# An attention backward kernel: K of nearly all heads is transposed by DMA, and V is loaded a tick sooner

## The chip, the cores and the metric

The kernel runs on one core of a Trainium2 chip. The metric is the device time of one execution in microseconds (us); the time before is the median of three runs, 1652.15 us (1651.94 to 1654.73). A core has TensorE (PE, matrix products), VectorE (DVE), ScalarE (ACT), GpSimd (POOL) and SyncE (SP). In this kernel SyncE issues all DMA transfers, one after the other, in one queue; sixteen DMA engines carry them out.

## The reference: what is computed

Two independent attention blocks, A and B, each with 8 batch elements, 32 heads, 96 query tokens, 512 cached keys and a head width of 128. The model width is 640. Their outputs are concatenated, and the gradient of the whole is taken for every input:

```python
q = (x @ wq).reshape(B, Sq, H, Dh).transpose(0, 2, 1, 3)
scores = jnp.einsum("bhqd,bhkd->bhqk", q, k_cache) * (Dh ** -0.5)
p = softmax(scores, axis=-1)
o = jnp.einsum("bhqk,bhkd->bhqd", p, v_cache)
out = o.transpose(0, 2, 1, 3).reshape(B, Sq, H * Dh) @ wo      # block A and block B
result = concatenate([outA, outB], axis=-1)
_out, _vjp = jax.vjp(_f, A_x, A_k_cache, A_v_cache, A_wq, A_wo, B_x, ...)
return (_out, *_vjp(grad_out))          # out, and dx, dk, dv, dwq, dwo of both blocks
```

All arrays are bfloat16. The caches K and V and their gradients make up most of the traffic: per head and pair of batch elements 256 KB each of K, V, dK and dV.

## The kernel before, in words

**Units and ticks.** The work is cut into units of one head h and one batch element b, 8 units per head, 512 in all. A unit passes through stages s1 to s8, and the stages of successive units are overlapped like in a pipeline. Time is counted in ticks: unit (h, b) has the tick ct = tick0 + 8h + b, and each of its stages runs at ct plus an offset from the table `OFF` (line 45). An `Emitter` (lines 16 to 28) collects all pieces as (tick, slot, function), sorts them, and emits them in that order; the order in which the pieces are emitted is the order of each engine's instructions, save that the softmax stages s2 and s3 are given a higher priority. A tick of TensorE lasts some 2.6 to 3.9 us, depending on what the heads add to it.

**The stages.**
- Load (`c_ld`, line 262): K and V of a pair of batch elements come by one plain DMA each. `OFF["ldk"]` is -5, `OFF["ldv"]` is -3. A pair is loaded at the tick of its even element, so K and V loads fall on odd ticks.
- Transposes (`c_xt`, line 272): K (`KT`) and V (`VT`) of the pair are needed with the head dimension on the partitions too. A DMA through the crossbar writes the transposed copy from SBUF to SBUF, at `OFF["kt"]` = -3 and `OFF["vt"]` = 0. It waits for the load.
- s1 (`c_s1`, line 280, at ct + 2): for some units K is transposed by TensorE instead, in four 128x128 pieces into PSUM (line 285), and VectorE copies the result to SBUF as `KT_pe` (line 287). Which units is told by `k_on_pe` (line 556): batch elements 0 and 1 of every even head, all of head 0 of both blocks, and all of head 1 of the first block.
- s2 (line 291, ct + 3): the scores S = Q K^T (line 298), their negated maximum on VectorE (line 300), and the exponential on ScalarE (line 310). s3: reciprocal of the row sum on VectorE (line 320), and the product `P_sb` on GpSimd (line 329).
- s4 (ct + 4): dV = P^T dO on TensorE (line 389), copied out by ScalarE into `dV_sb`; P is transposed. s5: O. s6 (ct + 6): dP = dO V^T (line 417), and dS on VectorE (line 421). s7 (ct + 7): dK (line 432), copied out by ScalarE (line 435), and dS transposed. s8 (ct + 8): dQ from K as loaded (line 340).
- Stores (`c_st`, line 395): dV of a pair at its odd element's ct + 5, dK at its ct + 8.

Between these units the heads' own work is spread: transposes and projections of wq and wo (`pA` to `pD`), gradients of wq and wo (`qA` to `qD`), and per group of up to five heads the output and dx projections (`gU`, line 514). A head with `gU` work in it takes longer than one without.

**SyncE's order.** Of the emitted pieces, the DMAs come to SyncE in the order of tick and slot: loads in slot 0, transposes in slot 1, stores in 1.5, weights in 1.6 and 1.7. So an odd tick holds a V load, a K load, a K transpose (if DMA does it) and a dK store; an even tick holds a V transpose and a dV store. Each waits in that queue for its data and for its buffer: the K load, for instance, for the matmuls that read the buffer last, which are those of s8. Whatever stands behind it in the queue waits too.

**Buffers.** K_sb has 7 buffers (of a pair each), V_sb 5, KT and VT 4 each, KT_pe 2, P_sb 5, dS_sb 3. The eight PSUM banks are shared by all products.

Of the kernel before, what the change touches and what calls it, by code (L numbers as in the profile page):

```python
# [11 lines left out]
BF16 = mybir.dt.bfloat16  # L12
# [29 lines left out]
SL_GRP = 95  # L42
SL_SETUP = 96

OFF = dict(ldk=-5, ldv=-3, kt=-3, vt=0, s2=3, s3=3, s4=4, s5=5, s6=6, s7=7, s8=8)
HK = dict(pA=-10, pA2=-9, pB=-3, pC0=[-2, 0], pC1=[-1, 0], pD1=1, pD0=2, qA0=18, qA1=17, qB=[19, 20], qD=[(18, 0, 2), (19, 2, 4), (21, 4, 5)])
EV = dict(pB0="act", pB1="dve", pC00="act", pC01="act", pC10="act", pC11="dve", pD0="dve", pD1="dve", qA0="act", qA1="dve", qB0="act", qB1="dve", qD="dve", gU="act")
GSPREAD0 = 9
# [2 lines left out]
SLOTS = dict(LOAD=0, S2A=5, S2B=5.5, S1=6, S8=10, S7=20, S5=30, S4=40, S6=50, S3A=52, S3B=53, S5B=54, HEAD=SL_HEAD, GRP=SL_GRP)  # L51


def build_block(tc, em, tick0, blk, x, kc, vc, wq, wo, g_all, out_all, dx, dk, dv, dwq, dwo, ident, ones, pools, HG=6, first=True, groups=None):
    nc = tc.nc
    B, Sq, D = x.shape
    _, H, Sk, Dh = kc.shape
# [6 lines left out]
    NB = 2  # L64
# [31 lines left out]
    const, ps, kvp, wk, hd, hst, grp = (pools[k] for k in ("const", "ps", "kvp", "wk", "hd", "hst", "grp"))  # L96

    def bank(shape, dt, name):
        return ps.tile(shape, dt, name=name, tag="bank")
# [11 lines left out]
    def pinned(ins):  # L111
        return tc.keep_in_program_order(ins)
# [149 lines left out]
    def c_ld(h, b, n, bufs):  # L262
        def f():
            src = kc if n == "K" else vc
            X = kvp.tile([128, NB, KC, 128], BF16, name=n + "_sb", bufs=bufs)
            pinned(nc.sync.dma_start(X[:], src[b:b + NB, h].rearrange("b (p c) d -> p b c d", c=KC)))
            for i in range(NB):
                st = CS.setdefault((blk, h, b + i), {})
                st[n + "_sb"], st[n + "_all"] = X[:, i], X
        return f  # L270
# [9 lines left out]
    def c_s1(h, b):  # L280
        def f():
            st = CS[(blk, h, b)]
            kT_ps = bank([128, Sk], BF16, "kT_ps")
            for c in range(KC):
                nc.tensor.transpose(kT_ps[:, c * 128:(c + 1) * 128], st["K_sb"][:, c, :], ident[:])
            KT = wk.tile([128, Sk], BF16, name="KT_pe", bufs=2)
            nc.vector.tensor_copy(KT[:], kT_ps[:])
            st["KT"] = KT[:]
        return f

    def c_s2a(h, b):
        def f():
            with tc.high_priority(PRIO_OFF):
# [3 lines left out]
                S_ps = bank([Sq, Sk], F32, "S_ps")  # L297
                nc.tensor.matmul(S_ps[:], hs["QT_h"][:, tok], st["KT"], start=True, stop=True)  # L298
                negm = wk.tile([Sq, 1], F32, name="negm", bufs=3)
# [24 lines left out]
    def c_s3b(h, b):  # L324
        def f():
            with tc.high_priority(PRIO_OFF):
                st = CS[(blk, h, b)]
                P_sb = wk.tile([Sq, Sk], BF16, name="P_sb", bufs=5)
                pinned(nc.gpsimd.tensor_scalar(P_sb[:], st["E_sb"][:], st["rinv"][:], 0.0, op0=ALU.mult, op1=ALU.add))  # L329
                st["P_sb"] = P_sb  # L330
        return f
# [79 lines left out]
    def c_s6(h, b):  # L411
        def f():
            st = CS[(blk, h, b)]
            hs = HS[(blk, h)]
            tok = slice(b * Sq, (b + 1) * Sq)
            dP_ps = bank([Sq, Sk], F32, "dP_ps")
            nc.tensor.matmul(dP_ps[:], hs["dOT_h"][:, tok], st["VT"], start=True, stop=True)  # L417
            dl_ps = bank([Sq, 1], F32, "dl_ps")
            nc.tensor.matmul(dl_ps[:], st["prod"][:], ones[:, 0:1], start=True, stop=True)  # L419
            dS_sb = wk.tile([Sq, Sk], BF16, name="dS_sb", bufs=3)  # L420
            nc.vector.scalar_tensor_tensor(dS_sb[:], dP_ps[:], dl_ps[:, 0:1], st["P_sb"][:], op0=ALU.subtract, op1=ALU.mult)  # L421
            st["dS_sb"] = dS_sb
        return f
# [130 lines left out]
    NTS = len(tsplits)  # L554

    def k_on_pe(h, b):
        return (b // NB == 0 and h % 2 == 0) or h == 0 or (first and h == 1)

    SX = pools["SX"]
    for g in range(NG):  # L560
        h0 = GH0[g]
        for hh in range(groups[g]):
            h = h0 + hh
            c0t = tick0 + h * B
            if not (first and h == 0):
                em.add(c0t + HK["pA"], SLOTS["LOAD"] + 1.7, pA(h))
                em.add(c0t + HK["pA2"], SLOTS["LOAD"] + 1.7, pA2(h))
            em.add(c0t + HK["pB"], SL_HEAD, pB(h))
            fh = first and h == 0
            p0, p1, d1, d0, late = HK["pC0"], HK["pC1"], HK["pD1"], HK["pD0"], 0  # L570
            if fh:
                p1, d1, d0, late = [3, 3], 3, 4, 7
            elif h == 0:
                p0, p1, d1, d0, late = [-2, 2], [0, 3], 3, 4, 7
            for si in range(NTS):
                em.add(c0t + p0[min(si, 1)], SL_HEAD, pC(h, 0, si))
                em.add(c0t + p1[min(si, 1)], SL_HEAD + late, pC(h, 1, si))
            em.add(c0t + d1, SL_HEAD + (8 if late else 0), pD(h, 1))
            em.add(c0t + d0, SL_HEAD, pD(h, 0))
            for b in range(B):  # L580
                ct = c0t + b
                if b % NB == 0:
                    em.add(tick0 - 12 if first and h == 0 and b == 0 else ct + OFF["ldk"], SLOTS["LOAD"], c_ld(h, b, "K", 7))
                    em.add(ct + OFF["ldv"], SLOTS["LOAD"], c_ld(h, b, "V", 5))
                    if not k_on_pe(h, b):
                        em.add(ct + OFF["kt"], SLOTS["LOAD"] + 1, c_xt(h, b, "KT", 4))
                    em.add(ct + OFF["vt"], SLOTS["LOAD"] + 1, c_xt(h, b, "VT", 4))
                if k_on_pe(h, b):
                    em.add(ct + 2, SLOTS["S1"], c_s1(h, b))
                em.add(ct + OFF["s2"], SLOTS["S2A"], c_s2a(h, b))  # L590
                em.add(ct + OFF["s2"], SLOTS["S2B"], c_s2b(h, b))
                em.add(ct + OFF["s3"], SLOTS["S3A"], c_s3a(h, b))
                em.add(ct + OFF["s3"], SLOTS["S3B"], c_s3b(h, b))
                em.add(ct + OFF["s5"], SLOTS["S5B"], c_s5b(h, b))
                if b % 2 == 1:
                    em.add(ct + OFF["s4"] + 1, SLOTS["LOAD"] + 1.5, c_st(h, b, "v"))
                    em.add(ct + OFF["s7"] + 1, SLOTS["LOAD"] + 1.5, c_st(h, b, "k"))
                em.add(ct + OFF["s4"], SLOTS["S4"], c_s4(h, b))
                for i, o in enumerate(("s8", "s7", "s5", "s4")):
                    SX.setdefault(ct + OFF[o], [None] * 4)[i] = (blk, h, b)  # L600
                em.add(ct + OFF["s6"], SLOTS["S6"], c_s6(h, b))
                em.add(ct + OFF["s7"], SLOTS["S7"], c_s7(h, b))
            hk = HK if first or h < H - 1 else dict(HK, qA0=13, qB=[14, 15], qA1=16, qD=[(19, 0, 2), (19, 2, 4), (19, 4, 5)])
            em.add(c0t + hk["qA0"], SL_HEAD, qA(h, 0))
            for di in range(len(wsplits)):
                em.add(c0t + hk["qB"][di], SL_HEAD + 1, qB(h, di))
            em.add(c0t + hk["qB"][-1] + 1, SLOTS["LOAD"] + 1.6, qB_st(h))
            em.add(c0t + hk["qA1"], SL_HEAD, qA(h, 1))
            for (k_, c_lo, c_hi) in hk["qD"]:
                if c_lo < DC and h % 2 == 1:  # L610
                    em.add(c0t + k_, SL_HEAD + 2, qD(h, c_lo, min(c_hi, DC)))
            if h % 2 == 1:
                em.add(c0t + hk["qD"][-1][0] + 1, SLOTS["LOAD"] + 1.6, qD_st(h))
        cLg = tick0 + (h0 + groups[g] - 1) * B + B - 1
        gs0 = max(3, (GSPREAD0 * groups[g]) // HG)
        gs1 = max(3, (GSPREAD1 * groups[g]) // HG)
        if not first and g == NG - 2:
            gs0, gs1 = 9, 9
        if g == 0:
            em.add(cLg + OFF["s5"] - 2, SL_LOAD, setup_acc)  # L620
        subs = [(0, t, gi) for t in range(TT) for gi in range(len(gsplits))] + [(1, t, gi) for t in range(TT) for gi in range(len(gsplits))]
        n_out = TT * len(gsplits)
        for i, (which, t, gi) in enumerate(subs):
            if which == 0:
                tk = cLg + OFF["s5"] + 2 + (i * gs0) // n_out
            else:
                tk = cLg + OFF["s8"] + 2 + gs0 - 3 + ((i - n_out) * gs1) // n_out
            em.add(tk, SL_GRP, gU(g, which, t, gi))
            if g == NG - 1 and gi == len(gsplits) - 1:
                em.add(tk + 1, SLOTS["LOAD"] + 1.6, gU_st(which, t))  # L630
# [124 lines left out]
```

## Time and profile before

| | before |
|---|---|
| median of 3 runs | 1652.15 us (1651.94 to 1654.73) |
| the profiled execution | 1653.38 us, its span 1651.2 us |
| granted TensorE clock, mean | 0.998 |
| busy, us: PE / ACT / DVE / POOL | 1633.2 / 1391.9 / 1283.2 / 527.9 |
| moved by DMA | 447.11 MB, 271 GB/s |
| transposes by DMA | 256 of V, 214 of K |
| units with K transposed by TensorE | 84 |

The span runs from the first to the last instruction of the profiled execution. "Busy" is the time in which at least one instruction of the engine was under way. A row of a timeline has the start in us from the span's start, the duration in us, the engine, the line, the operation, and what it writes and reads; "x4" says that four were merged, and brackets tell idle time before it and what ended it. SPq is SyncE's queue: its duration is how long SyncE was held at that instruction, with any wait, not how long the transfer took. "To landing" is the time from the issue to the moment at which the data were there. Matmul durations hold the way through the array, so those of successive matmuls overlap. PEld are weight loads beside the matmuls.

### The profile page before, as it was taken

To read this page: it belongs to the slowest core of one execution; us is meant where nothing else is said; L and a number is where in the kernel's file an instruction comes from. 1 tells how busy PE (TensorE), PEld (TensorE's weight loads), DVE (VectorE), ACT (ScalarE), POOL (GpSimd) and SP (SyncE) were. 2 spreads that over 40 slices of the span, in tenths; PEclk is the share of its full clock that TensorE was granted. 3 is DMA by queue.
4 is the path that set the end of the run, shared out by engine and by line. 5 is a ranking of instruction groups with operands and counts; after the bars stand their busy time and mean duration, and the time that the engine had idled before them with its cause. 6 is when DMAs were issued, how large, how long until landed. Compare 5 with 4: busy or idle time off the path is not lost.

```text
span 1651.2 us, 55679 instructions
## 1 busy us (share of the span) xinstructions
PE 1633.2 (99%) x21288; PEld 1303.0 (79%) x21288; DVE 1283.2 (78%) x2916; ACT 1391.9 (84%) x3518; POOL 527.9 (32%) x1034
## 2 busy tenths in 40 slices
PE   8999999999999999999999999999999999999999
PEld 6887787788788787887878877877877877877886
DVE  6886677788787787878878767778878778787777
ACT  6998898798798797988869998978977977987985
POOL 2332233232233232333323323323322322332332
PEclk9999999999999999999999999999999999999999
DMA  9999999999999999999999999999999999999995
GB/s 258 270 268 283 277 284 271 279 274 283 246 277 269 276 273 264 267 278 259 299 289 283 283 281 272 278 281 271 276 275 260 278 296 246 282 282 245 265 275 157
DMA packets 843947, 447.11 MB, mean 271 GB/s; under 512 B 516512, under 2 KB 843680, under 8 KB 843680
## 3 DMA queue, kind: packets, MB, share of 16 engines
q1 hardware_dynamic: 843680, 443.56, 110.8%
q8 instruction: 167, 2.74, 0.7%
q14 instruction: 100, 0.82, 0.1%
HBM read 161.09 MB, written 159.12 MB: 194 GB/s over the span
## 4 chain that ended last, share of the span: by engine, by line
PE 74%; ACT 15%; issue 5%; DVE 3%; DMA 2%; POOL 0%; SPq 0%; ACTq 0%; DVEq 0%; POOLq 0%
PE o_ps L514 12%; PE q_ps L243 10%; PE dwq_ps L490 6%; PE dK_ps L432 5%; PE dV_ps L389 5%; PE dP_ps L417 5%; PE S_ps L298 5%; PE dwo_ps L469 4%; PE dst_ps L346 4%; PE x_ps L365 4%; PE x_ps L359 4%; PE x_ps L340 4%; ACT dK_sb L435 3%; ACT E_sb L310 3%; ACT PT_sb L378 3%
## 5 line engine op out<-in xcount | busy, mean ns | idle before, releaser
L329 POOL TENSOR_SCALAR P_sb<-E_sb,rinv 96x512 bf16<-96x512 bf16 x512 | 353.6, 691 | 1096.3 <-DVE rinv L320 1062.1
L310 ACT ACTIVATE E_sb<-S_ps,negm 96x512 bf16<-96x512 f32 x512 | 354.4, 692 | 132.7 <-DVE negm L300 128.9
L421 DVE SCALAR_TENSOR_TENSOR dS_sb<-dP_ps,dl_ps,P_sb 96x512 bf16<-96x512 f32 x512 | 380.9, 744 | 46.7 <-PE dl_ps L419 42.4
L300 DVE TENSOR_REDUCE negm<-S_ps 96x1 f32<-96x512 f32 x512 | 347.5, 679 | 46.0 <-PE S_ps L298 43.9
L435 ACT ACTIVATE dK_sb<-dK_ps 128x512 bf16<-128x512 f32 x512 | 305.7, 597 | 89.1 <-PE dK_ps L432 88.1
L392 ACT ACTIVATE dV_sb<-dV_ps 128x512 bf16<-128x512 f32 x512 | 314.6, 614 | 0.0
L378 ACT ACTIVATE PT_sb<-x_ps 128x384 bf16<-128x384 bf16 x512 | 256.4, 501 | 0.0
L514 PEld LDWEIGHTS <-OD 128*128 128x128 bf16 x1536 | 135.7, 98 | 103.3 <-issue 1.3
L389 PE MATMUL dV_ps<-dOnat_h,P_sb 96*128 96x128 bf16 x2048 | 197.9, 219 | 1.0 <-DVE dOnat_h L160 0.6
L432 PE MATMUL dK_ps<-Qnat_h,dS_sb 96*128 96x128 bf16 x2048 | 197.8, 219 | 0.0
L417 PE MATMUL dP_ps<-VT,dOT_h 128*96 128x512 bf16 x512 | 195.3, 381 | 0.3
L407 POOL TENSOR_TENSOR prod<-OD,dOT_h 128x96 bf16<-128x96 bf16 x512 | 186.6, 364 | 9.2 <-ACT OD L375 8.2
L348 DVE COPY dST_sb<-dst_ps 128x384 bf16<-128x384 bf16 x512 | 177.1, 346 | 11.6 <-PE dst_ps L346 11.6
L320 DVE RECIPROCAL rinv<-rowsum 96x1 f32<-96x1 f32 x512 | 80.0, 156 | 133.3 <-ACT E_sb L310 128.6
L375 ACT ACTIVATE OD<-x_ps 128x192 bf16<-128x192 f32 (+1 forms) x515 | 171.4, 333 | 3.4 <-PE x_ps L340 3.4
L346 PE MATMUL dst_ps<-ident,dS_sb 96*128 96x96 bf16 x2048 | 171.8, 206 | 2.4 <-DVE dS_sb L421 0.2
L359 PE MATMUL x_ps<-PT_sb,V_sb 128*128 128x96 bf16 x2048 | 172.2, 206 | 0.5 <-ACT PT_sb L378 0.5
L365 PE MATMUL x_ps<-ident,P_sb 96*128 96x96 bf16 x2048 | 171.7, 205 | 0.5 <-POOL P_sb L329 0.3
L340 PE MATMUL x_ps<-dST_sb,K_sb 128*128 128x96 bf16 x2048 | 170.7, 206 | 0.0
L298 PE MATMUL S_ps<-KT,QT_h 128*96 128x512 bf16 x428 | 162.1, 379 | 1.1 <-DMA KT<-K_sb 0.7
L340 PEld LDWEIGHTS <-K_sb 128*128 128x128 bf16 x2048 | 133.3, 98 | 34.6
L514 PE MATMUL o_ps<-wo_h,OD 128*128 128x128 bf16 (+1 forms) x768 | 141.0, 299 | 0.0
(75 smaller groups left out, 3137.9 us busy)
## 6 DMA issues: line engine op xcount, KB each, us to landing
out_dram<-dV_sb SPq DMA_DIRECT2D x256, 256.0 KB, 3.5
out_dram<-dK_sb SPq DMA_DIRECT2D x256, 256.0 KB, 3.8
K_sb<-in_A_k_cache_dram SPq DMA_DIRECT2D x128, 256.0 KB, 4.1
V_sb<-in_A_v_cache_dram SPq DMA_DIRECT2D x128, 256.0 KB, 3.8
K_sb<-in_B_k_cache_dram SPq DMA_DIRECT2D x128, 256.0 KB, 4.1
V_sb<-in_B_v_cache_dram SPq DMA_DIRECT2D x128, 256.0 KB, 4.0
out_dram<-dwo_sb SPq DMA_DIRECT2D x64, 160.0 KB, 3.8
out_dram<-dwq_sb SPq DMA_DIRECT2D x32, 320.0 KB, 4.0
```

What stands on the lines that cost most here:

```text
L300: nc.vector.tensor_reduce(negm[:], S_ps[:], axis=AX.X, op=ALU.max, negate=True)
L310: nc.scalar.activation(E_sb[:], st["S_ps"][:], ACT.Exp, bias=st["negm"][:], scale=1.0, accum_out=rowsum[:])
L329: pinned(nc.gpsimd.tensor_scalar(P_sb[:], st["E_sb"][:], st["rinv"][:], 0.0, op0=ALU.mult, op1=ALU.add))
L340: nc.tensor.matmul(dQT_ps, st["K_sb"][:, c, :], st["dST_sb"][:, c * Sq:(c + 1) * Sq], start=(c == 0), stop=(c == KC - 1))
L378: nc.scalar.activation(PT_sb[:], PT_ps, ACT.Identity, scale=1.0)
L389: nc.tensor.matmul(dV_ps[:, c * 128:(c + 1) * 128], P_sb[:, c * 128:(c + 1) * 128], hs["dOnat_h"][:, b * 128:(b + 1) * 128], start=True, s ...
L392: nc.scalar.activation(SB[(blk, h, b // 2, "v")][:, b % 2], dV_ps[:], ACT.Identity, scale=1.0)
L417: nc.tensor.matmul(dP_ps[:], hs["dOT_h"][:, tok], st["VT"], start=True, stop=True)
L421: nc.vector.scalar_tensor_tensor(dS_sb[:], dP_ps[:], dl_ps[:, 0:1], st["P_sb"][:], op0=ALU.subtract, op1=ALU.mult)
L432: nc.tensor.matmul(dK_ps[:, c * 128:(c + 1) * 128], dS_sb[:, c * 128:(c + 1) * 128], hs["Qnat_h"][:, b * 128:(b + 1) * 128], start=True, s ...
L435: nc.scalar.activation(SB[(blk, h, b // 2, "k")][:, b % 2], dK_ps[:], ACT.Identity, scale=1.0)
L514: nc.tensor.matmul(o_ps[:], src[:, t * 128:(t + 1) * 128], rhs, start=(hh == 0), stop=(hh == groups[g] - 1))
```

## The change

1. `k_on_pe` is cut down: TensorE transposes K only in head 0 of both blocks and in head 1 of the first. The two units of every other even head, which it transposed too, now get K by a DMA transpose, one more per even head.
2. V is loaded at ct - 4 instead of ct - 3, and V_sb has 6 buffers instead of 5. The V load now falls on an even tick. SyncE's order becomes: odd tick K load, K transpose, dK store; even tick V load, V transpose, dV store. So two plain transfers stand between any two transposes (weights and their gradients aside), where it was one and three.
3. KT_pe has 1 buffer instead of 2, P_sb 4 instead of 5, dS_sb 2 instead of 3.

```diff
-OFF = dict(ldk=-5, ldv=-3, kt=-3, vt=0, s2=3, s3=3, s4=4, s5=5, s6=6, s7=7, s8=8)
+OFF = dict(ldk=-5, ldv=-4, kt=-3, vt=0, s2=3, s3=3, s4=4, s5=5, s6=6, s7=7, s8=8)
...
-            KT = wk.tile([128, Sk], BF16, name="KT_pe", bufs=2)
+            KT = wk.tile([128, Sk], BF16, name="KT_pe", bufs=1)
...
-                P_sb = wk.tile([Sq, Sk], BF16, name="P_sb", bufs=5)
+                P_sb = wk.tile([Sq, Sk], BF16, name="P_sb", bufs=4)
...
-            dS_sb = wk.tile([Sq, Sk], BF16, name="dS_sb", bufs=3)
+            dS_sb = wk.tile([Sq, Sk], BF16, name="dS_sb", bufs=2)
...
     def k_on_pe(h, b):
-        return (b // NB == 0 and h % 2 == 0) or h == 0 or (first and h == 1)
+        return h == 0 or (first and h == 1)
...
-                    em.add(ct + OFF["ldv"], SLOTS["LOAD"], c_ld(h, b, "V", 5))
+                    em.add(ct + OFF["ldv"], SLOTS["LOAD"], c_ld(h, b, "V", 6))
```

## The prediction

> **What bounds the kernel now.** I read the page first, then the table of waits (last line: total us, times, longest), then TensorE's timeline, then SyncE's.
>
> ```profile
> span 1651.2 us, 55679 instructions
> PE 1633.2 (99%) x21288; PEld 1303.0 (79%) x21288; DVE 1283.2 (78%) x2916; ACT 1391.9 (84%) x3518; POOL 527.9 (32%) x1034
> PEclk9999999999999999999999999999999999999999
> ...
> PE 74%; ACT 15%; issue 5%; DVE 3%; DMA 2%; POOL 0%; SPq 0%; ACTq 0%; DVEq 0%; POOLq 0%
> ...
> PE S_ps L298 <- DMA KT<-K_sb: 0.7, 1, 0.7
> ```
>
> TensorE is busy for 99% of the span and carries 74% of the chain; the clock is granted in full, and TensorE waited for a K transpose only once. So TensorE is the bound, and a matmul taken away is worth its slot in TensorE's stream. The slot is not the duration that a group shows, because the durations overlap. It is the distance to the next start (columns: start in us, duration):
>
> ```profile
> 203.88 0.39 PE L285 MATMUL kT_ps<-ident,K_sb 128*128 128x128 bf16 x4
> 204.10 0.25 PE L340 MATMUL x_ps<-dST_sb,K_sb 128*128 128x96 bf16 x2
> ...
> L285 PE MATMUL kT_ps<-ident,K_sb x336: 216/219/219, 12.1 to 1574.2; 128*128 128x128 bf16 x168
> L287 DVE COPY KT_pe<-kT_ps x84: 397/408/425, 12.5 to 1575.5; 128x512 bf16<-128x512 bf16 x84
> ```
>
> Four transposes for one batch element lie 204.10 - 203.88 = 0.22 us in front of the next work, not 4 x 0.219 us.
>
> Behind TensorE stands a second line of work that is nearly as long: SyncE's one queue. The starts of the first K load of heads 8, 9, 10, 11 and 12 in that queue are these:
>
> ```profile
> 184.24 0.44 SPq L266 DMA_DIRECT2D K_sb<-in_A_k_cache_dram  x1
> 208.24 0.44 SPq L266 DMA_DIRECT2D K_sb<-in_A_k_cache_dram  x1
> 233.54 0.45 SPq L266 DMA_DIRECT2D K_sb<-in_A_k_cache_dram  x1
> 257.69 0.45 SPq L266 DMA_DIRECT2D K_sb<-in_A_k_cache_dram  x1
> 282.67 0.44 SPq L266 DMA_DIRECT2D K_sb<-in_A_k_cache_dram  x1
> ...
> VT<-V_sb SPq DMA_TRANSPOSE x16, 4.5
> KT<-K_sb SPq DMA_TRANSPOSE x14, 5.0
> ```
>
> The queue takes 24.00, 25.30, 24.15 and 24.98 us per head. The even heads have 7 transposes by DMA, the odd ones 8 (14 + 16 = 30 in the four). The mean is 24.61. TensorE's pace over 60 heads comes from the score matmul of batch element 2, in head 2 and in head 62, and the K transposes of these have the issue and the landing time beside them:
>
> ```profile
> 62.24 0.38 PE L298 MATMUL S_ps<-KT,QT_h 128*96 128x512 bf16 x1
> 1578.40 0.38 PE L298 MATMUL S_ps<-KT,QT_h 128*96 128x512 bf16 x1
> ...
> 47.91 1.23 SPq L275 DMA_TRANSPOSE KT<-K_sb  x1
> KT<-K_sb SPq DMA_TRANSPOSE x1, 3.5
> ```
>
> That is (1578.40 - 62.24) / 60 = 25.27 us per head. The queue has 0.66 us to spare per head, and at head 2 the K transpose lands at 51.4, 10.8 us ahead of its use. I call this distance the lead. It is spent in heads where TensorE is quick and won back in heads that carry the output projections. Its low points, as issue, landing time and use, in heads 5, 10, 37 and 42:
>
> ```profile
> 115.89 1.23 SPq L275 DMA_TRANSPOSE KT<-K_sb  x1
> KT<-K_sb SPq DMA_TRANSPOSE x1, 6.1
> 122.62 0.38 PE L298 MATMUL S_ps<-KT,QT_h 128*96 128x512 bf16 x1
> ...
> 252.62 1.25 SPq L275 DMA_TRANSPOSE KT<-K_sb  x1
> KT<-K_sb SPq DMA_TRANSPOSE x1, 5.6
> 261.80 0.38 PE L298 MATMUL S_ps<-KT,QT_h 128*96 128x512 bf16 x1
> ...
> 932.64 1.68 SPq L275 DMA_TRANSPOSE KT<-K_sb  x1
> KT<-K_sb SPq DMA_TRANSPOSE x1, 5.6
> 938.25 0.42 PE L298 MATMUL S_ps<-KT,QT_h 128*96 128x512 bf16 x1
> ...
> 1064.44 1.26 SPq L275 DMA_TRANSPOSE KT<-K_sb  x1
> KT<-K_sb SPq DMA_TRANSPOSE x1, 4.3
> 1071.56 0.38 PE L298 MATMUL S_ps<-KT,QT_h 128*96 128x512 bf16 x1
> ```
>
> The leads are 0.6, 3.6, 0.0 and 2.8 us. In head 37 nothing is left already.
>
> **The change part by part.** *K off TensorE.* On TensorE, K of batch elements 0 and 1 is transposed in every even head, and all of the first heads: 84 units (the row of L287). Left are head 0 of both blocks and head 1 of the first, 24 units. So 60 units go: 60 x 0.22 = **13.2 us** off TensorE, 0.44 per even head. Also 60 copies of 0.408 = 24.5 us go off VectorE; VectorE is busy for 78% and carries 3% of the chain, so I count them at nothing. They would count where VectorE ends the wait for TensorE, which the profile shows for short stretches only.
>
> *Thirty transposes more in the queue*, one per even head. Neighbouring passes differ by 25.30 - 24.00 = 1.30 and 24.98 - 24.15 = 0.83; the mean over the four passes is 1.07 us, and I take it. This is a price for the queue with everything behind it (issue, back-pressure, transfer), since it is read off the distance between loads.
>
> One rule speaks against moving a transpose to DMA at all. The Trainium skill, "VectorE: DVE Perf Modes", section "The three transpose paths", puts a 128x128 bf16 transpose at 390 ns on TensorE and 1309 ns on the DMA crossbar, and its rules prefer TensorE where PSUM can take the result. One transfer here holds eight such blocks, which by that figure would be an estimate of 10.5 us each and 314 us for thirty, and the kernel would be far slower. The trace doesn't bear that out: here the whole of such a transfer lands in 3.5 to 6.1 us and costs the queue 1.07.
>
> *What the lead does then.* Per even head the queue loses 1.07 us and TensorE gains 0.44, so the lead shrinks by 1.51 us per even head since it was last full or empty. Head 5: two transposes more (heads 2, 4), 3.0 - 0.6 = 2.4 us of stall. Head 10: from empty at 5 it had won 3.6 - 0.6 = 3.0; three more transposes take 4.5; stall 1.5. Head 37: two more (34, 36), all 3.0 stall. Head 42: won 2.8, three more take 4.5; stall 1.7. Together 8.6 us. With 0.83 as the price (1.27 per even head) it is 1.9 + 0.8 + 2.5 + 1.0 = 6.2; with 1.30 (1.74) it is 2.9 + 2.2 + 3.5 + 2.4 = 11.0. SyncE still makes small waits of its own in such stretches, which would be used up first:
>
> ```profile
> SPq L266 <- PE dK_ps L432: 83.0, 81, 3.6
> ```
>
> They are 1.0 us each. I take off one in each of the two stretches that begin empty (heads 5 to 10, 37 to 42): 8.6 - 2.0 = **6.6 us** of stalls, in which TensorE waits for the K transpose.
>
> *V loads a tick sooner, with a sixth buffer.* 256 loads move in SyncE's order past the next K load, one K transpose and one dK store. Before, dK's store alone lay between a K transpose and the V transpose after it, and three plain transfers before the next K transpose; afterwards it is two and two. No transfer is added. The V transpose gets a tick more behind its load, which it doesn't need. What the order is worth, the trace can only bound, by how long SyncE is held at an issue (min/median/max ns):
>
> ```profile
> L275 SPq DMA_TRANSPOSE KT<-K_sb x214: 1231/1236/2621, 47.9 to 1605.8; - x107
> L275 SPq DMA_TRANSPOSE VT<-V_sb x256: 1231/1384/3427, 12.2 to 1611.0; - x128
> ```
>
> The V transpose, with one plain transfer in front, takes 0.15 us longer. Either both get the shorter issue (0.15 less per pair of batch elements, 0.6 per head), or both the longer one (0.6 more per head). Halfway between one and three, I take zero, and keep both ends for the range.
>
> *Fewer buffers* (KT_pe 2 to 1, P_sb 5 to 4, dS_sb 3 to 2). Each adds a wait for the reader of an earlier one.
>
> ```profile
> 206.08 0.74 DVE L421 SCALAR_TENSOR_TENSOR dS_sb<-dP_ps,dl_ps,P_sb 96x512 bf16<-96x512 f32 x1
> 208.58 0.69 POOL L329 TENSOR_SCALAR P_sb<-E_sb,rinv 96x512 bf16<-96x512 bf16 x1 [1.88 <-DVE rinv L320]
> ...
> 13.02 0.38 PE L298 MATMUL S_ps<-KT_pe,QT_h 128*96 128x512 bf16 x1 [0.52 <-DVE KT_pe L287]
> 14.04 0.41 DVE L287 COPY KT_pe<-kT_ps 128x512 bf16<-128x512 bf16 x1
> ```
>
> The P_sb that would reuse the buffer starts at 208.58, after its last reader ended at 206.82: 1.8 us of room on GpSimd. KT_pe has 14.04 - 13.40 = 0.6 us, and only first heads still use it. dS_sb is rewritten two ticks on and last read one tick on. I count all three at zero; the cover is that room, and if it went, the score chain behind P_sb would slip by the difference each tick.
>
> *Sum:* -13.2 + 6.6 = -6.6 us. The profiled execution took 1653.38 us with a span of 1651.2; its span becomes 1644.6. The median of the runs, 1652.15, lies 1.2 below that execution; taken off it, the sum makes 1645.6, so **1646**.
>
> **The rivals.** *The lead suffices (faster in full).* If the even order gives both transposes the short issue, the queue passes a head in 24.61 + 0.53 - 0.6 = 24.54 us, against TensorE's 25.27 - 0.22 = 25.05. No stall is left: 1652.15 - 13.2 = 1639. For it: the K transposes with three plain transfers in front are the quick ones. Against it: nothing shows that two do as well.
>
> *The queue becomes the bound (slower).* Without any help the queue needs 24.61 + 0.53 = 25.14 per head against 25.05: it is level, and each tenth on the queue then counts 60 times. With both transposes at the long issue it is 25.74, 60 x 25.74 = 1544 against the 1516 of before, less the 10.8 us of lead that can be spent once: 17 us slower, 1669. It decides from about 25.45 per head on ((1516 + 10.8) / 60), 0.3 more than I reckon: there the gain is gone. The rule of the Trainium skill in "VectorE: DVE Perf Modes", cited above, would end on this side too, by a much larger amount.
>
> *TensorE isn't what ends those ticks.* Around the removed transposes of head 40, the chain of that stretch runs over ScalarE:
>
> ```profile
> by line: ACT dK_sb L435 17.2%; issue 16.2%; ACT dV_sb L392 15.3%; ACT PT_sb L378 12.6%; ACT E_sb L310 10.4%; ACT OD L375 8.4%; ACT Onat L157 6.6%; PE dK_ps L432 2.5%; PE dV_ps L389 2.5%; PE dP_ps L417 2.4%; ACT dwo_sb L157 2.3%; PE dst_ps L
> ```
>
> If half of the 13.2 us came to nothing there, the lead would shrink by 1.29 instead of 1.51 per even head; the same four points give 2.0 + 0.9 + 2.6 + 1.1 - 2.0 = 4.6 us of stalls: 1652.15 - 6.6 + 4.6 = 1650, no change. Against it: TensorE shows hardly a gap.
>
> **How the numbers follow.** Forecast (1640 to 1648.5) 0.37, lead suffices 0.18, ScalarE ends the ticks 0.20, queue the bound 0.25. About 0.2% (3.3 us) is what a measurement of this kernel can tell from no change. Of the forecast and the full gain 0.50 lies below 1648.8 and 0.05 just above; the third rival lies within 0.2%; the queue rival above 1655.5. Faster 0.50, same 0.25, slower 0.25. The range runs from 1638, just under the full gain, to 1662, in the queue rival's middle, as an order that costs a little would pull all heads along; the likeliest case alone would have 1640 to 1649.
>
> **What would show it.** Right: the K transposes of TensorE are 96 instead of 336 and KT by DMA 244 instead of 214; waits of S_ps for KT<-K_sb grow from 0.7 us to some 7, around heads 4 to 10 and 36 to 42; head passes of SyncE in even heads are as long as in odd ones, near 25.2; the issue medians of KT and VT move together. Wrong: if those waits reach 20 us and more, or passes of 25.7, the queue has become the bound; if they stay at 1 us and the time is 1639, the order paid; if neither waits nor order moved and the time is still 1651, another engine ended those ticks.

## The result, and the profile after

The changed kernel took 1643.21 us (median of four runs, 1642.49 to 1643.39) against 1652.05 for the kernel before on the same chip. The ratio is 0.9939, with a 95% interval of 0.9927 to 0.9951. That is 8.8 us less by the medians and 10.1 by the ratio. The profiled execution took 1643.09 us.

The first rows are of the page of the changed kernel: span, busy times, and the shares of the chain of waits.

```profile
span 1641.3 us, 55280 instructions
...
PE 1621.3 (99%) x21048; PEld 1289.1 (79%) x21048; DVE 1268.2 (77%) x2856; ACT 1388.7 (85%) x3518; POOL 526.7 (32%) x1034
...
PE 81%; ACT 10%; DVE 4%; issue 3%; DMA 2%; SPq 0%; POOL 0%; ACTq 0%; DVEq 0%; POOLq 0%
```

TensorE is still the bound, and carries more of the chain than before (81% after 74%). Its table of waits in the changed kernel (total us, times, longest) has what was to grow, and two rows that the forecast did not have:

```profile
PE dst_ps L346 <- ACT PT_sb L378: 3.6, 21, 0.2
PE S_ps L298 <- ACT E_sb L310: 2.7, 17, 0.2
...
PE S_ps L298 <- DMA KT<-K_sb: 0.8, 2, 0.6
```

The waits for K, 0.7 us before, are 0.8 us now. The two rows on ScalarE did not exist before. The rows of the transposes in the changed kernel (count, min/median/max ns, first and last start) show that the change did what it says, and what SyncE's issues became:

```profile
L285 PE MATMUL kT_ps<-ident,K_sb x96: 217/219/219, 10.3 to 829.9; 128*128 128x128 bf16 x96
```
```profile
L275 SPq DMA_TRANSPOSE KT<-K_sb x244: 1231/1391/2798, 40.1 to 1593.6; - x122
```
```profile
L275 SPq DMA_TRANSPOSE VT<-V_sb x256: 1231/1236/2493, 11.8 to 1600.4; - x128
```

The medians did not move together: K's went from 1236 to 1391 ns, V's from 1384 to 1236. They changed places.

**How much of it is the change.** The 9.9 us between the two spans are not all of it. The weight load of the score matmul runs once per unit, 512 times, so its first and last start frame the whole pipeline. Before, and then after:

```profile
L298 PEld LDWEIGHTS <-QT_h x512: 119/123/124, 12.4 to 1621.4; 128*96 128x96 bf16 x171
```
```profile
L298 PEld LDWEIGHTS <-QT_h x512: 119/123/124, 10.6 to 1611.6; 128*96 128x96 bf16 x171
```

Before, 1621.4 - 12.4 = 1609.0 us; after, 1611.6 - 10.6 = 1601.0. The pipeline gained **8.0 us**. The other 1.8 us lie ahead of its first unit, where TensorE waits for the first x. Of the seven traces (those below included) with V loaded at ct - 3, three begin the pipeline at 12.4 us and four between 10.4 and 11.2, whatever the rest of the kernel; the seven others begin it between 10.3 and 10.6. So I take the 1.8 us for a start that comes out one way or the other, and leave it out of the account. This is not shown: the kernel before has one trace only (of the changed one there are two, which begin at 10.6 and 10.5). Below, "the pipeline" is the distance from the first to the last of these weight loads.

**Where the 8.0 us are.** In head 10, the starts of the score matmuls of the unit before it and of its first five (batch elements 0 to 4), before and then after:

```profile
247.33 0.38 PE L298 MATMUL S_ps<-KT,QT_h 128*96 128x512 bf16 x1
250.00 0.38 PE L298 MATMUL S_ps<-KT_pe,QT_h 128*96 128x512 bf16 x1
252.53 0.38 PE L298 MATMUL S_ps<-KT_pe,QT_h 128*96 128x512 bf16 x1
...
257.54 0.38 PE L298 MATMUL S_ps<-KT,QT_h 128*96 128x512 bf16 x1
261.80 0.38 PE L298 MATMUL S_ps<-KT,QT_h 128*96 128x512 bf16 x1
```
```profile
244.82 0.38 PE L298 MATMUL S_ps<-KT,QT_h 128*96 128x512 bf16 x1
247.40 0.38 PE L298 MATMUL S_ps<-KT,QT_h 128*96 128x512 bf16 x1
249.83 0.38 PE L298 MATMUL S_ps<-KT,QT_h 128*96 128x512 bf16 x1 [0.16 <-ACT E_sb L310]
...
254.84 0.38 PE L298 MATMUL S_ps<-KT,QT_h 128*96 128x512 bf16 x1
259.20 0.38 PE L298 MATMUL S_ps<-KT,QT_h 128*96 128x512 bf16 x1
```

Each of the first two ticks held one removed transpose of 0.22 us. They went from 2.67 to 2.58 and from 2.53 to 2.43: 0.19 us instead of 0.44. The tick from element 3 to 4 then went from 4.26 to 4.36, so 0.10 of that was given back. (Ticks here last from 2.4 to 4.4 us, a wider range than the 2.6 to 3.9 named for the kernel before.) The next views are the busy times in these two ticks, before and then after (stretch; length; PE, PEld, DVE, ACT, POOL with instructions; then clock, DMA share and GB/s); under them stands ScalarE's part in the second tick after:

```profile
247.33:250.00 2.67, 2.67 (x48) 2.48 (x47) 2.67 (x7) 2.53 (x9) 1.14 (x3) 1.00 1.32 166
250.00:252.53 2.53, 2.48 (x42) 2.21 (x41) 2.53 (x7) 2.53 (x7) 0.75 (x2) 1.00 1.09 307
```
```profile
244.82:247.40 2.58, 2.58 (x45) 2.33 (x44) 2.58 (x7) 2.43 (x8) 1.04 (x3) 1.00 1.18 320
247.40:249.83 2.43, 2.27 (x37) 1.91 (x35) 2.12 (x5) 2.43 (x7) 0.84 (x2) 1.00 1.48 252
```
```profile
248.30 0.82 ACT L157 ACTIVATE Onat<-nat_ps 128x768 bf16<-128x768 bf16 x1
248.99 0.70 ACT L310 ACTIVATE E_sb<-S_ps,negm 96x512 bf16<-96x512 f32 x1
```

In the second tick ScalarE is busy for all of the 2.43 us, TensorE for 2.27. The score matmul of element 1 writes a PSUM bank that the exponential `E_sb` must have read first; that ends at 248.99 + 0.70 = 249.69, and the matmul starts at 249.83. So in this tick ScalarE is what TensorE comes up against. The first tick has no such wait, and here it is VectorE that is busy for all of the 2.58 us, with ScalarE at 2.43. VectorE was busy for all of both ticks before, too, though its share of the whole span was 78%. So two engines are level with TensorE here, and what ends the first tick is not shown.

The starts of all 512 score matmuls, taken apart in this way, give three kinds among the 30 even heads that lost their transposes. In the 18 that have no output projection in these two ticks (heads 2, 4, 8, 10 and so on; 17 of them have the wait for `E_sb`), the two ticks gain some 0.19 and the tick from 3 to 4 mostly gives 0.10 back. In the heads with projection matmuls there (line 514), TensorE has more to do: five gain 0.45, the slot in full, three about 0.37, and four 0.83, more than the slot. (In head 12, one of these four, TensorE was busy for 3.21 of the second tick's 3.38 us before, and for all of its 2.88 after; so waits went with the transposes.) Over the 30 heads the two ticks gained 10.0 us instead of 13.2, and the tick from 3 to 4 gave back 2.7, some 0.8 of it in head 36, where TensorE waits for K.

### The profile page after: what moved, and what is told of

It reads as the page before. It is cut to its first block, busy times and chain, and to the rows that moved or that the text cites. A ratio compares the mean times of both kernels' runs of the same rounds, so it can differ in the third digit from the quotient of the medians.

```text
span 1641.3 us, 55280 instructions
## 1 busy us (share of the span) xinstructions
PE 1621.3 (99%) x21048; PEld 1289.1 (79%) x21048; DVE 1268.2 (77%) x2856; ACT 1388.7 (85%) x3518; POOL 526.7 (32%) x1034
## 4 chain that ended last, share of the span: by engine, by line
PE 81%; ACT 10%; DVE 4%; issue 3%; DMA 2%; SPq 0%; POOL 0%; ACTq 0%; DVEq 0%; POOLq 0%
PE q_ps L243 13%; PE o_ps L514 12%; PE dwq_ps L490 6%; PE dP_ps L417 6%; PE dK_ps L432 6%; PE dV_ps L389 5%; PE S_ps L298 5%; PE dst_ps L346 5%; PE dwo_ps L469 4%; PE x_ps L365 4%; PE x_ps L359 4%; PE x_ps L340 4%; ACT E_sb L310 3%; ACT dK_sb L435 2%; PE n_ps L258 2%
## 5 line engine op out<-in xcount | busy, mean ns | idle before, releaser
L298 PE MATMUL S_ps<-KT,QT_h 128*96 128x512 bf16 x488 | 184.7, 379 | 3.9 <-ACT E_sb L310 2.7
L348 DVE COPY dST_sb<-dst_ps 128x384 bf16<-128x384 bf16 x512 | 177.2, 346 | 14.0 <-PE dst_ps L346 13.2
```

## The experiments

Each is a small edit of the kernel before or of the changed one. "Ratio" is to the kernel before on the same chip. Two views are used throughout: the pipeline's length, and SyncE's pass, the time that its queue takes for a head, with whatever it waits for. The pass is read where the queue is behind, between the first K loads of heads 35 and 43. Before, changed, and e1 (changed without the new order):

```profile
876.44 0.46 SPq L266 DMA_DIRECT2D K_sb<-in_B_k_cache_dram  x1
1075.84 0.45 SPq L266 DMA_DIRECT2D K_sb<-in_B_k_cache_dram  x1
```
```profile
872.33 0.41 SPq L266 DMA_DIRECT2D K_sb<-in_B_k_cache_dram  x1
1068.99 0.42 SPq L266 DMA_DIRECT2D K_sb<-in_B_k_cache_dram  x1
```
```profile
877.74 0.45 SPq L266 DMA_DIRECT2D K_sb<-in_B_k_cache_dram  x1
1080.87 0.45 SPq L266 DMA_DIRECT2D K_sb<-in_B_k_cache_dram  x1
```

199.40, 196.66 and 203.13 us for eight heads: passes of 24.93, 24.58 and 25.39 us. All results together, with the profiled execution's pipeline and pass:

| kernel | median us | ratio (95%) | pipeline us | pass us |
|---|---|---|---|---|
| before | 1652.05 | 1 | 1609.0 | 24.93 |
| changed | 1643.21 | 0.9939 (0.9927 to 0.9951) | 1601.0 | 24.58 |
| e1, K by DMA in the old order | 1659.47 | 1.0038 (1.0020 to 1.0056) | 1611.7 | 25.39 |
| e2, new order alone | 1650.92 | 0.9986 (0.9976 to 0.9995) | 1608.4 | 24.60 |
| e3, K's transposes left out | 1645.55 | 0.9958 (0.9942 to 0.9974) | 1602.2 | 24.61 |
| e4, fewer buffers alone | 1653.31 | 0.9993 (0.9979 to 1.0007) | 1610.2 | 24.98 |
| e5, V two ticks sooner | 1656.25 | 1.0013 (0.9997 to 1.0029) | 1613.2 | 25.50 |
| e6, K sooner instead of V | 1643.54 | 0.9943 (0.9926 to 0.9960) | 1600.4 | 24.70 |
| e7, transposes adjacent | 1763.70 | 1.0680 (1.0644 to 1.0715) | 1718.1 | 26.86 |
| e8, Onat to VectorE | 1641.73 | 0.9933 (0.9918 to 0.9947) | 1598.9 | 24.60 |
| e9, dV store moved | 1665.68 | 1.0068 (1.0049 to 1.0086) | 1622.4 | 25.48 |
| e10, changed again | 1642.94 | 0.9940 (0.9925 to 0.9954) | 1600.8 | 24.46 |
| e11, e8 again | 1642.31 | 0.9935 (0.9922 to 0.9948) | 1600.2 | 24.64 |
| e12, Onat and dQ's copy swapped | 1641.82 | 0.9934 (0.9921 to 0.9947) | 1600.1 | 24.57 |

A short pass isn't the queue's need alone. These are the first K loads of heads 35 and 43 in e2 and then in e3:

```profile
874.44 0.41 SPq L266 DMA_DIRECT2D K_sb<-in_B_k_cache_dram  x1
1071.28 0.44 SPq L266 DMA_DIRECT2D K_sb<-in_B_k_cache_dram  x1
```
```profile
874.18 0.46 SPq L266 DMA_DIRECT2D K_sb<-in_B_k_cache_dram  x1
1071.04 0.45 SPq L266 DMA_DIRECT2D K_sb<-in_B_k_cache_dram  x1
```

The queues of e3 and e4 hold the same transfers in the same order as before, and pass in 24.61 and 24.98. The queue of e2 has the changed kernel's order with four transposes fewer in these eight heads, and passes no faster (24.60 against 24.58). So a pass of some 24.6 tells the most that the queue needs, and not how much it needs. The four passes above 25.3 (e1, e5, e7, e9) belong to the traces in which TensorE waits longest for K.

**e1: K by DMA, in the old order.** The changed kernel with the V loads put back.

```diff
-OFF = dict(ldk=-5, ldv=-4, kt=-3, vt=0, ...)
+OFF = dict(ldk=-5, ldv=-3, kt=-3, vt=0, ...)
-                    em.add(ct + OFF["ldv"], SLOTS["LOAD"], c_ld(h, b, "V", 6))
+                    em.add(ct + OFF["ldv"], SLOTS["LOAD"], c_ld(h, b, "V", 5))
```

> K of all heads but the first by DMA as in the changed kernel, with the smaller buffers, but V loaded where it was before (ct - 3, 5 buffers): the order of one and three plain transfers stays. Theory 'the order pays' (the queue's pass per head is 0.6 to 0.7 us shorter by the even order; a transpose costs about 1.07): passes of SyncE near 25.2 us in every head, stalls of TensorE for the K transpose of 6 us and more around heads 5 to 10 and 36 to 42, time 1646 to 1650 us. Rival 'transposes are nearly free, the order does nothing': passes near 24.4, the same waits and the same time as the changed kernel, 1643 us.

It took 1659.47 us, slower than before, and its times scatter (1651.56 to 1668.57). In the table of waits of e1:

```profile
PEld L298 <- DMA KT<-K_sb: 9.4, 8, 3.3
...
PE S_ps L298 <- DMA KT<-K_sb: 7.0, 5, 3.1
```

The sum is near the 6.6 us that the prediction forecast for the change, but nearly all of it lies in heads 36 to 42, as the same table for 870 to 1090 us shows:

```profile
PE S_ps L298 <- DMA KT<-K_sb: 6.7, 4, 3.1
```

Head 5 has the other 0.3. The profiled execution took 1654.66 us, 4.8 below the median, so the slower executions may well wait longer. The pass lengthened from 24.93 to 25.39 for half a transpose more per head (heads 36 to 42 have four in eight heads): 203.13 - 199.40 = 3.73 us, 0.93 for each. Against e3 and e4, whose queues hold what that of before holds, it is 1.57 and 0.82; one trace each fixes the price no better than that. The changed kernel differs from this one in the order and in a sixth V buffer; e5 has that buffer and the order of one and three. The passes differ by 25.39 - 24.58 = 0.81 us per head, the medians by 16 us.

**e2: the new order alone.** The changed kernel with K of the even heads back on TensorE.

```diff
-        return h == 0 or (first and h == 1)
+        return (b // NB == 0 and h % 2 == 0) or h == 0 or (first and h == 1)
```

> V loads a tick sooner, six V buffers and the smaller other buffers, but K of batch elements 0 and 1 in even heads stays on TensorE. 'The order pays': SyncE passes an odd head in 24.6 us (25.3 before) and an even one, with 7 transposes, in 23.6 when it runs freely; TensorE's work is that of before, so the time is 1651 to 1652 us, with no wait for a K transpose left. 'The order does nothing': passes of 25.3 and 24.1 as before, 1652 us. The time alone does not tell the two apart, the passes do.

1650.92 us, 0.14% less than before; the pipeline is 0.6 us shorter. The row of e2 for the score matmul's wait on K is gone; that wait was 0.7 us. The passes, which were to tell the two readings apart, don't: 24.60 us here, but 24.61 in e3 with the old order. The order of a queue is worth next to nothing as long as TensorE doesn't wait for it. The order pays only together with the transposes that it makes room for.

**e3: K's transposes left out.** The kernel before with the three smaller buffer counts, in which the 58 units with K on TensorE (first heads and head 2 aside) are not transposed at all: neither the four matmuls nor the copy, and no DMA in their place.

```diff
     def c_s1(h, b):
         def f():
             st = CS[(blk, h, b)]
+            if not (h == 0 or (first and h <= 2)):
+                st["KT"] = CS[(blk, h - 1, 6 + b)]["KT"]
+                return
```

> Order and number of DMA transposes as before, smaller buffers; the K transposes on TensorE and their copies on VectorE are left out in even heads from head 4 of the first block and head 2 of the second on (58 of the 60 units), and the scores of these units use the transposed K of the pair before, so this part of the computation is left out and the result is another. It measures what TensorE's 58 x 0.22 = 12.8 us are worth with no transfer added. 'TensorE's stream is the bound': 1652 - 12.8 = 1639 us, plus some 1 to 2 us for a lead that shrinks by 0.44 per even head. 'ScalarE takes part of it back' (waits of the score matmul for a PSUM bank that the exponential frees): 1642 to 1643, about what the changed kernel has.

This measures the disputed term by itself. By 58 x 0.22 it is 12.8 us; against the 1652.90 that the kernel before took beside it, the median gives 1652.90 - 1645.55 = 7.4 (by the interval, 4.3 to 9.6), and the pipeline 1609.0 - 1602.2 = 6.8. Its row, to be held against those above:

```profile
L301 PEld LDWEIGHTS <-QT_h x512: 119/123/134, 12.4 to 1614.6; 128*96 128x96 bf16 x171
```

The same two rows on ScalarE stand in its table of waits, though nothing was added to any queue:

```profile
PE dst_ps L349 <- ACT PT_sb L381: 3.3, 19, 0.2
PE S_ps L301 <- ACT E_sb L313: 2.4, 15, 0.2
```

So nearly half of the time that TensorE was spared did not come, with or without the DMA transposes. (The lines are three further on, because of the edit.)

**e4: fewer buffers alone.** The kernel before with KT_pe 1, P_sb 4, dS_sb 2.

```diff
-name="KT_pe", bufs=2   -name="P_sb", bufs=5   -name="dS_sb", bufs=3
+name="KT_pe", bufs=1   +name="P_sb", bufs=4   +name="dS_sb", bufs=2
```

> The kernel before with KT_pe 1, P_sb 4 and dS_sb 2 buffers, nothing else. Theory (each has 0.6 to 1.8 us of room): 1652 us, the same as before within 0.1%. Rival (a tighter buffer costs some of the gain that is missing, 1639 against 1643): 1654 to 1656.

0.9993, with 1 inside the interval. The smaller counts cost nothing that can be told from 0.14% either way.

**e5: V two ticks sooner.** The changed kernel with the V load at ct - 5. It falls on an odd tick again, and the plain transfers between transposes are one and three as before.

```diff
-OFF = dict(ldk=-5, ldv=-4, ...)
+OFF = dict(ldk=-5, ldv=-5, ...)
```

> The changed kernel with V loaded at ct - 5 instead of ct - 4: the load comes still earlier, but falls on an odd tick again, so the order is one and three plain transfers. Theory 'the order pays': passes of SyncE near 25 us per head instead of 24.4, waits for K transposes of some 10 to 16 us, time as with the old order, 1650 to 1660. Rival 'the earlier V load pays': passes of 24.4, time 1643 or less.

1656.25 us and a pass of 25.50, like e1. V sooner isn't what helps; the order is.

**e6: K sooner instead of V.** The changed kernel with K loaded at ct - 6 in 8 buffers, and V back at ct - 3 in 5. Two plain transfers stand between any two transposes, again a load and a store, but others.

```diff
-OFF = dict(ldk=-5, ldv=-4, ...)    -c_ld(h, b, "K", 7)   -c_ld(h, b, "V", 6)
+OFF = dict(ldk=-6, ldv=-3, ...)    +c_ld(h, b, "K", 8)   +c_ld(h, b, "V", 5)
```

> Two plain transfers between any two transposes, made in another way: V loads as before (ct - 3, 5 buffers), K loads a tick sooner (ct - 6, 8 buffers), so that K loads fall on even ticks. 'The order pays': passes of 24.4 us and 1643 us, as in the changed kernel, within 2 us. 'The earlier V load pays': passes of 25, 1650 or more.

1643.54 us, a pass of 24.70: the changed kernel's time by another way.

**e7: transposes adjacent.** The changed kernel with the V transpose a tick sooner (5 buffers of VT) and the V load at ct - 3 with 5 buffers. VT and KT now stand side by side, and four plain transfers follow them.

```diff
-OFF = dict(ldk=-5, ldv=-4, kt=-3, vt=0, ...)    -c_ld(h, b, "V", 6)   -c_xt(h, b, "VT", 4)
+OFF = dict(ldk=-5, ldv=-3, kt=-3, vt=-1, ...)   +c_ld(h, b, "V", 5)   +c_xt(h, b, "VT", 5)
```

> The uneven order driven further: V transposes at ct - 1 (5 VT buffers, V loads at ct - 3 with 5), so that the K and the V transpose stand side by side, and four plain transfers stand between them and the next pair. 'The order pays', by how uneven it is: passes some 0.6 us longer again than with one and three, 25.6 us in every head, 15 to 25 us of waits for the K transpose, 1660 to 1670. Rival 'the number between does not matter, something else in the old order did': passes of 24.4 to 25 and 1643 to 1652.

1763.70 us, 6.8% slower. The K transpose, second of the two, now holds SyncE for 1990 ns in the median (1391 in the changed kernel), and TensorE waits for K again and again. From the rows of the tile and of the waits of e7:

```profile
L275 SPq DMA_TRANSPOSE KT<-K_sb x244: 1265/1990/4914, 41.7 to 1714.1; - x122
```
```profile
PEld L298 <- DMA KT<-K_sb: 98.8, 60, 3.8
PE S_ps L298 <- DMA KT<-K_sb: 82.9, 51, 3.5
```

With the same transfers as in the changed kernel, this order makes 120 us.

**e8: Onat to VectorE.** In the changed kernel ScalarE ends the second of the shortened ticks, and `Onat` (0.82 us, once per head) stands in it. Here VectorE does that copy.

```diff
-EV = dict(..., qA0="act", qA1="dve", ...)
+EV = dict(..., qA0="dve", qA1="dve", ...)
```

> The changed kernel with the copy of Onat (0.82 us per head) on VectorE instead of ScalarE. Theory 'ScalarE took back part of the gain in the very ticks in which TensorE became shorter' (in even heads the score matmuls of batch elements 0 and 1 wait some 0.1 and 0.3 us for the PSUM bank that the exponential, queued behind this copy, frees): these waits shrink from about 8 us to under 3, and the time falls by 2 to 5 us, to 1638 to 1641. Rival 'VectorE is as full there': the waits move to dS and its readers, time 1643 or more.

1641.73 us; the wait of S_ps for `E_sb` is gone and that of dst_ps for `PT_sb` is down to 0.5 us:

```profile
PE dst_ps L346 <- ACT PT_sb L378: 0.5, 3, 0.2
PE S_ps L298 <- DMA KT<-K_sb: 0.5, 1, 0.5
```

The chain moves from ScalarE (10% to 4%) to VectorE (4% to 7%). The pipeline is 2.1 us shorter than the changed kernel's. But the two shortened ticks gained nothing: over the 30 even heads they are 9.8 us shorter than before, against 10.0 in the changed kernel. This is the second of them in head 10:

```profile
247.12:249.55 2.43, 2.39 (x39) 2.14 (x36) 2.43 (x6) 2.12 (x6) 0.84 (x2) 1.00 0.70 233
```

It lasts 2.43 us as before the move, and now VectorE is busy for all of it and ScalarE for 2.12. So ScalarE alone isn't what limits this tick.

**e9: the dV store moved.** A test of the reading that it is the number of plain transfers between transposes that counts. The changed kernel with V loaded at ct - 3, and the dV store a tick later, behind the dK store. The order is K transpose, dK store, dV store, V transpose, V load, K load: two and two, but stores together and loads together.

```diff
-OFF = dict(ldk=-5, ldv=-4, ...)    -c_ld(h, b, "V", 6)
+OFF = dict(ldk=-5, ldv=-3, ...)    +c_ld(h, b, "V", 5)
-                    em.add(ct + OFF["s4"] + 1, SLOTS["LOAD"] + 1.5, c_st(h, b, "v"))
+                    em.add(ct + OFF["s4"] + 2, SLOTS["LOAD"] + 1.55, c_st(h, b, "v"))
```

> Two plain transfers between any two transposes, made by moving a store and no load: V loads as before (ct - 3, 5 buffers), the dV store one tick later, behind the dK store. The order is K transpose, dK store, dV store, V transpose, V load, K load: even in number, but stores stand with stores and loads with loads. Theory 'the number between two transposes decides': passes near 24.5 us per head, 1643 us. Rival 'a store beside a load decides' (what the changed kernel and the sooner K loads have in common): passes near 25.2, 1650 us or more.

1665.68 us, and a pass of 25.48 from these two rows:

```profile
886.12 0.46 SPq L266 DMA_DIRECT2D K_sb<-in_B_k_cache_dram  x1
1089.95 0.43 SPq L266 DMA_DIRECT2D K_sb<-in_B_k_cache_dram  x1
```

So two and two is not enough for a short pass. The time of e9 is not a clean measure, though: ScalarE waits for a `dV_sb` buffer until the later store has read it, which the changed kernel and e1 don't have.

```profile
ACT dV_sb L392 <- DMA out_dram<-dV_sb: 17.8, 19, 2.6
```

What the changed kernel and e6 share, and e1, e5, e7 and e9 don't, is a store beside a load between any two transposes. They share something else as well: a load stands directly ahead of every transpose, where in the other four one of the two transposes follows a store or a transpose. The runs don't tell these two readings apart, and why such an order is cheaper stays open.

**e10 and e11: the changed kernel and e8 again, side by side.** To tell whether the 1.5 us of e8 are real.

> The changed kernel as it is, for a comparison on the same chip: 1643 us, 0.994 of the kernel before.

> The changed kernel with the copy of Onat on VectorE, once more beside the changed one: 1.5 to 2 us faster than it (1641 to 1642) if the waits for the exponential's bank are what it loses; the same as it if the first comparison was chance.

1642.94 and 1642.31 us. The intervals of the ratios lie over each other; the pipelines are 1600.8 and 1600.2. The gain of e8 is not shown. The wait for `E_sb` is gone in e8 and e11, and little comes of it. By the starts of the score matmuls, against the changed kernel, the even heads' tick from element 1 to 2 gains 2.4 us in all, that from 2 to 3 gives 3.4 back, and that from 3 to 4 gains 4.0 to 4.1; the even heads gain 2.7 to 2.9 us in all, and the other heads lose 0.9 to 1.8.

**e12: swapped.** `Onat` goes to VectorE and the copy of dQ (`qA1`) to ScalarE, so that both engines keep their load.

```diff
-EV = dict(..., qA0="act", qA1="dve", ...)
+EV = dict(..., qA0="dve", qA1="act", ...)
```

> Onat's copy on VectorE and dQnat's on ScalarE (a tick earlier): VectorE has 0.54 us per head less than in the kernel with Onat's copy alone moved, ScalarE 0.8 more. If VectorE's fullness is what still holds TensorE there (waits for dS), 1 to 2 us faster than that kernel, 1640; if ScalarE is the tighter one, its waits return, 1643.

1641.82 us, with an interval that takes in e10's ratio. The waits for `E_sb` and `PT_sb` are as small as in e8. No version here is shown to beat the changed kernel.

## Why the prediction was right, and where its steps were not

It said 1646 us, with a range of 1638 to 1662, and faster as the likelier sign. Measured were 1643.2. The sum came out 2.8 us off, but two of its terms were off by more, on opposite sides.

*K off TensorE, -13.2 us:* mis-sized. The slot of 0.22 us came in full in five heads, 0.45 per even head. But 18 of 30 heads gained 0.19 instead of 0.44 in the shortened ticks, and gave half of that back. e3 measures the term at 6.8 to 7.4. The step that failed is the one that let a slot in TensorE's stream count in full because TensorE is busy for 99%: a second engine can be level with it in some ticks and far behind in others. The third rival named this mechanism, and its "half of the 13.2 us" is what e3 shows. It named ScalarE, and that is shown in part only: ScalarE ends the second tick, but with `Onat` moved off it (e8, e11) the two ticks are no shorter, and VectorE is then busy for all of both (head 10). Which engine would have to give, and how much, stays open. What the rival had against it, that TensorE shows hardly a gap, was no evidence: before, the K transposes filled the gap.

*VectorE's copies at nothing:* not tested apart, as e3 leaves out the transposes and the copies together. VectorE's busy time fell by 1283.2 - 1268.2 = 15.0 us. Its mean of 78% and its 3% of the chain were no ground for nothing: it was busy for all of the two ticks in question.

*Thirty transposes at 1.07 us:* 0.82 to 1.57 in e1, by which trace it is held against. The forecast lies between, but it was read from four passes alone (heads 8 to 12), and these scatter: in e4, with the same transfers in the same order, they are 26.8, 25.6, 25.3 and 25.1 us, and the even heads are no shorter.

*Stalls of 6.6 us:* the sum is right for the old order, and in part by luck. e1 has 7.0 us of them on the score matmul, but 0.3 around heads 5 to 10, where some 2.9 were forecast, and 6.7 in heads 36 to 42 instead of 3.7. In the changed kernel they are 0.8.

*The order at zero:* this is the step that failed there. The two ends were -0.6 and +0.6 us per head; between e1 and the changed kernel it is -0.81. The issue medians were the wrong witness: K's and V's changed places, which would say no gain at all, while the pass of the whole queue shortened. How long SyncE is held at one kind of issue doesn't tell how long the pass is.

*Fewer buffers at zero:* nothing that e4 can tell from zero.

*The rivals.* "The lead suffices" was right that the order pays and that no stalls to speak of are left; that its pass of 24.54 is near the 24.58 measured is in part luck, as e2 passes in 24.60 with fewer transposes. It missed the time, as it too let 13.2 us count in full. "The queue becomes the bound" is what would have come without the order: e1 was slower than before (1.0038), and e7 shows how far it can go. The rule of the Trainium skill cited there, "VectorE: DVE Perf Modes", section "Rules for kernel authors", prefers TensorE for a 128x128 transpose where PSUM can take the result. With the old order the runs agree (e1, 1.0038); with the changed one they don't (0.9939), where eight such blocks cost the queue some 0.8 to 1.6 us and TensorE is the bound.

*Together:* the changed kernel is two rivals at once, the order of the first and the lost half of the third: about -7 from TensorE, with stalls that stayed below 1 us. So 1646 came out as the difference of two terms that were both too large, by some 6 us each, and its nearness to 1643.2 is in good part luck. The pipeline shows -8.0; the 1 us between this and -7 lies within what two traces of one kernel differ by (e8 and e11: 1598.9 and 1600.2).

*What was to show it:* 96 transposes on TensorE and 244 by DMA came; waits of some 7 us did not; passes near 25.2 did not; the medians did not move together.

## What to carry to other kernels

A matmul taken off the bounding engine is worth its slot only in those stretches where no other engine is level with it; look at the busy times of all engines in the very ticks that get shorter, and not at the mean over the span. Leave the work out altogether in one run, as e3 does: it measures the gain with no new cost in it. In a single DMA queue with transposes and plain transfers, try the order of the issues before giving up on a transfer that doesn't fit: here the same transfers took between 24.5 and 26.9 us per head.

## What the runs showed of the hardware that was not expected

*The order of the issues.* The same 16 plain transfers and 8 transposes per head passed in 24.46 to 24.70 us (six traces) with a store and a load between any two transposes, in 25.39 to 25.50 (three) with the order one and three or with stores together and loads together, and in 26.86 (one) with transposes side by side.

*The transfers pause, all at once.* The GB/s row of the changed kernel between 700 and 712 us (40 slices of 0.3 us; a packet's bytes count where it starts) shows it, and under it stand the packets of instruction fetches in these 12 us (number, MB, share):

```profile
GB/s 350 331 389 307 304 115 0 0 5 9 13 264 48 10 318 386 384 388 388 372 304 286 32 19 275 338 386 386 389 386 271 334 264 7 4 9 9 165 386 372
q14 instruction: 2, 0.02, 1.3%
q8 instruction: 2, 0.03, 1.0%
```

Four times in 12 us the rate falls from some 260 to 390 GB/s to under 50, for 0.6 to 1.5 us. SyncE issued transposes at 698.55, 703.90, 706.39 and 708.95, but the second pause begins at 703.6, before the issue next to it, and fetches of instructions run in the same stretch. So it is not shown that the transposes make the pauses. In e7, the row for 735 to 748 us (slices of 0.325 us) has a longer one:

```profile
GB/s 31 6 9 9 25 17 235 279 310 267 12 8 110 391 381 404 371 384 381 388 378 391 336 290 291 279 276 315 109 0 2 9 9 287 384 388 378 385 394 372
```

There SyncE was held for 3.84 us at the K transpose issued at 733.16, and the engines moved next to nothing from 735.0 to 736.95:

```profile
733.16 3.84 SPq L275 DMA_TRANSPOSE KT<-K_sb  x1
```

What the transfers wait for in these pauses, and whether the order of the issues changes their number, was not settled by these runs.
